# A fused attention and gMLP block on one core: stage-1 loads by need on the SP queue, four-deep key rings, small results on ScalarE

## The chip, the core and the metric

The kernel runs on one core of one Trainium2 chip. The core has five engines with an instruction queue each: TensorE (PE, matmuls; PEld is its weight load), VectorE (DVE), ScalarE (ACT), GpSimd (POOL) and SyncE (SP, which here only issues transfers). ACT can issue transfers too. Transfers run on 16 DMA engines, in one queue row for SP (q1 in the profile) and one for ACT (q10). SBUF is the memory on the core, PSUM holds matmul results. The metric is the device time of one execution in microseconds. Before the change it is 290.84 us, the median of 3 runs (290.23 to 293.64).

## The reference

S = 2048 rows, D = 448, 16 heads of 28, F = 1792; inputs in bfloat16. A condition vector c gives six modulation vectors. Part A is linear attention with softmax features, part B a gMLP with a 2048 x 2048 mixing matrix along the rows.

```python
mod = (_silu(c) @ w_mod).reshape(c.shape[0], 6, 1, -1)      # sa, ca, ga, sb, cb, gb
h = _layernorm(x) * (1 + ca) + sa
q, k, v = heads(h @ wqkv)
phi_k = concat([softmax(k @ w_phi), softmax(-(k @ w_phi))]) # the same for q
kv = einsum('bhsf,bhsd->bhfd', phi_k, v); z = phi_k summed over s
o = (phi_q @ kv) / (phi_q . z + 1e-06)
x = x + ga * (o @ wo)
h = _layernorm(x) * (1 + cb) + sb
zz = _gelu(h @ w_in); z1 = first half; z2 = _layernorm(second half)
g = einsum('ts,bsf->btf', w_sp, z2) + b_sp[None, :, None]
x = x + gb * ((z1 * g) @ w_out)
```

## The kernel before

The rows are 16 tiles of 128. All work stands in one hand-written order; each engine executes its own instructions in that order and waits by semaphores. A second, general path behind a flag is not taken.

**Constants and weights.** The key weights are transposed on PE (`fold_T`, L677), multiplied by w_phi (`fold_pf`, L697) and scaled by 1 + ca on the way out of PSUM (ca1, the second result of `colform`, L708, which multiplies a modulation matrix by silu(c)). `fold_sa` (L689) adds the shift sa as one more column of the transposed weights, copied out by DVE at L695. The same is done for the query weights inside the loop (`late`, L878). `keep_busy` (L624) runs matmuls whose result nobody reads.

**Stage 1**, the loop of L909. For key tile i: `k_part` (L769) multiplies hT (the normalised x, transposed) by the key weights, ACT takes exp(k) and exp(-k) into a ring E of three (L774, L775); `v_part` (L777) does the values, copied by ACT into a second ring; `k_norm` (L783) on DVE sums, inverts and multiplies (L786, L789, L790) into a third ring; `kv_acc` (L794) of tile i-2 adds to the accumulator kvacc in PSUM. For tiles ahead, `l1_stats(i + 6)` (L658) takes mean and variance, on DVE up to tile 9 and on ACT from 10 on; POOL computes the inverse root and applies it (`l1_apply(i + 5)`, L672), and SP transposes the tile by a transfer into hT (L651). `loads(i)` (L843) issues one load per tile on ACT's queue. `late(i)` places the query weights (tiles 1 to 3), the second modulation (tile 5: `one_plus(colform(wm1, 1), cb1)`, then a second `colform`, both in the same PSUM buffer, read by DVE at L717 and L892), the bias products of w_in (`win_bias`, tiles 7 and 8), its scaling on DVE (`win_scale`, tiles 9 to 12) and the gate. Query products `q_mm` (L802) stand behind tiles 9 and 12, and `q_one` (L817) behind the loop; ACT takes exp of both signs.

**PSUM.** Tag B has four banks, tag A two double banks. kvacc holds one of tag A through stage 1. A product waits until the bank that it gets has been read out.

**Stage 2**, `slot(j)` of L1061, j from 0 to 22. In slot j PE makes the attention product of tile j (`num_mm`), DVE finishes tile j-1 (`num_fin`, L972: five operations from L977 to L985, after ACT has copied two sums, `num_sx`, L970), POOL and SP bring it transposed to PE, `wo_mm(j-3)` multiplies by wo and adds x, DVE takes the statistic (L634), POOL applies it for tile j-4 (h2T), and `z2_mm(j-5)` multiplies by the second half of w_in; ACT takes the gelu (L1046) and DVE the statistic (L1008) one slot later. From slot 9 on the first half, `z1`, is multiplied too. The loads of w_sp (`load_wsp`, L826) are transposing transfers on SP, placed in tiles 12 to 14 and slots 5 to 15. The six last `q_one` stand in slots 0 to 5.

**The mixing**, `g_unit` (L1128): 448 matmuls over w_sp, and the output products `o_mm` (L1137), until the end.

## Time and profile before

| | |
|---|---|
| median of 3 runs | 290.84 us (290.23 to 293.64) |
| the profiled execution | 294.1 us, span 292.2 us |
| PE busy | 265.7 us (91%) |
| DVE, ACT, POOL busy | 161.5, 117.2, 90.5 us |
| mean granted clock of PE | 0.948 |

The page cuts the span into 40 equal slices of 7.3 us. Each digit is a share in tenths; PEclk is the granted clock of PE in tenths of full speed (the two levels are 1.2 and 2.4 GHz), DMA the busy share of the 16 DMA engines. Up to slice 15 PE and its clock are uneven, from there on PE is full.

### The profile page before, as it was taken

The page shows a single profiled execution, that of the slowest core. Times are in us where ns is not written, and L with a number is a line of the kernel's source. Part 1 is how long each engine was busy: PE and PEld are TensorE (multiplying, and loading weights), DVE is VectorE, ACT ScalarE, POOL GpSimd, SP SyncE. Part 2 cuts the span into 40 slices and gives each one's busy share as a digit, 9 for nine tenths or more (in the row PEclk, how much of TensorE's full clock was granted, in tenths as well). Part 3 has the DMA queues.
Part 4 walks back from the last instruction along what each step waited for, and adds up shares of the span by engine and source line. Part 5 has one row for each costly group of instructions (what it writes and reads, how often), then busy time and mean ns, then how long its engine had stood idle before and what let it go on. Part 6 is the DMA issues. An engine that isn't in the chain of part 4 may idle for free.

```text
span 292.2 us, 4412 instructions
## 1 busy us (share of the span) xinstructions
PE 265.7 (91%) x1567; PEld 134.3 (46%) x1567; DVE 161.5 (55%) x341; ACT 117.2 (40%) x237; POOL 90.5 (31%) x197
## 2 busy tenths in 40 slices
PE   6795959999995799997999999999999999999991
PEld 3543535556552345554544444444444444444440
DVE  4839645589677489896854324443434353435251
ACT  2347468988972567875788820000000000000000
POOL 3848531330047376774764560000000000000000
PEclk9669777999999789999999999999999999999998
DMA  7679946639012448479734999100000001000002
GB/s 181 154 154 287 160 127 146 92 61 158 0 36 56 91 94 123 96 179 197 109 73 110 185 183 195 17 0 16 18 31 0 16 16 34 0 16 18 31 5 69
DMA packets 71233, 25.82 MB, mean 88 GB/s; under 512 B 61281, under 2 KB 71074, under 8 KB 71202
## 3 DMA queue, kind: packets, MB, share of 16 engines
q1 hardware_dynamic: 63682, 17.79, 33.1%
q10 hardware_dynamic: 7520, 7.66, 10.0%
...
## 4 chain that ended last, share of the span: by engine, by line
PE 58%; DMA 2%; DVE 2%; ACT 1%; issue 1%; ACTq 0%; DVEq 0%
PE g_ps L1132 33%; PE o_ps L1139 7%; PE z_ps L1053 7%; PE z_ps L1040 7%; PE x_ps L998 2%; DMA h2T<-f_xpad 2%; PE num L962 1%; ACT f_z2n L1031 1%; DVE t L985 1%; PE x_ps L996 1%; ACT f_z1T L1054 0%; DVE stats L1008 0%; DVE num L981 0%; DVE cr L977 0%; DVE w L983 0%
## 5 line engine op out<-in xcount | busy, mean ns | idle before, releaser
L1132 PE MATMUL g_ps<-f_wsp,f_z2n 128*128 128x512 bf16 x336 | 74.3, 379 | 0.0
L1132 PEld LDWEIGHTS <-f_z2n 128*128 128x128 bf16 x448 | 43.8, 98 | 52.0
L1134 DVE TENSOR_TENSOR gb<-g_ps,f_bsp 128x512 f32<-128x512 f32 x28 | 19.4, 692 | 70.7 <-PE g_ps L1132 70.7
L1184 ACT CAST ot<-o_ps 128x224 bf16<-128x224 f32 x1 | 0.3, 346 | 116.7 <-PE o_ps L1139 116.7
L1040 PE MATMUL z_ps<-f_win,h2T 128*128 128x448 bf16 (+1 forms) x128 | 28.3, 364 | 4.4 <-DVE t L985 2.6
L1053 PE MATMUL z_ps<-h2T,f_win 128*128 128x512 bf16 x112 | 26.4, 379 | 0.0
L987 POOL TENSOR_TENSOR f_opad<-t 128x448 bf16<-128x448 bf16 x16 | 16.6, 1034 | 27.3 <-DVE t L985 27.3
L1132 PE MATMUL g_ps<-f_hT,f_z2n 128*128 128x512 bf16 x112 | 25.0, 379 | 0.0
L786 DVE TENSOR_REDUCE sums<-f_E 128x32 f32<-128x896 bf16 x16 | 17.2, 1074 | 12.3 <-ACT f_E L775 12.3
L1008 DVE BATCH_NORM_STATS2 stats<-z2g 128x6 f32<-128x448 bf16 x32 | 18.4, 615 | 9.7 <-ACT z2g L1046 9.6
L1139 PE MATMUL o_ps<-f_wout,f_z1T 128*128 128x448 bf16 x112 | 23.5, 352 | 0.0
L1135 DVE TENSOR_TENSOR f_z1T<-gb,f_z1T 128x512 bf16<-128x512 f32 x28 | 19.7, 704 | 1.4
L1046 ACT ACTIVATE z2g<-z_ps 128x896 bf16<-128x896 f32 x16 | 14.7, 918 | 13.0 <-PE z_ps L1040 13.0
L780 PE MATMUL v_ps<-f_Wv,f_hT 128*128 128x448 bf16 x64 | 16.5, 387 | 3.5 <-DVE f_wTq L695 3.5
L1040 PEld LDWEIGHTS <-h2T 128*128 128x128 bf16 (+1 forms) x128 | 12.1, 99 | 15.5 <-issue 3.7
L772 PE MATMUL k_ps<-f_Wk,f_hT 128*128 128x448 bf16 x64 | 18.0, 412 | 1.0 <-DMA f_hT<-f_xpad 0.5
L1031 ACT ACTIVATE f_z2n<-z2g,nm,rs 128x896 bf16<-128x896 bf16 x16 | 18.1, 1132 | 1.6 <-POOL nm L1018 1.4
L985 DVE TENSOR_TENSOR t<-num,w 128x896 bf16<-128x896 f32 x16 | 17.5, 1091 | 1.5
L1053 PEld LDWEIGHTS <-f_win 128*128 128x128 bf16 x112 | 10.9, 97 | 12.6
L998 PE MATMUL x_ps<-f_wo,oT 128*128 128x448 bf16 x64 | 15.6, 369 | 0.8 <-DMA oT<-f_opad 0.8
L824 ACT ACTIVATE f_Eq<-q_ps 112x512 bf16<-112x512 f32 x24 | 12.6, 598 | 8.9 <-PE q_ps L821 8.8
L1139 PEld LDWEIGHTS <-f_z1T 128*128 128x128 bf16 x112 | 11.0, 98 | 10.9
...
## 6 DMA issues: line engine op xcount, KB each, us to landing
...
f_x<-in_A_x_dram ACTq DMA_DIRECT2D x2, 448.0 KB, 4.6
...
```

Source lines behind the costliest of these rows:

```text
L772: nc.tensor.matmul(k_ps[:, 0:D], lhsT=hT[0:KB[kc], kc, i * P:(i + 1) * P], rhs=Wk[0:KB[kc], kc, 0:D], start=(kc == 0), stop=(kc == KC - 1))
L786: nc.vector.tensor_reduce(out=sums[:], in_=E[:].rearrange("p s (c f h) -> p (s c) h f", c=4, h=HP), axis=AX.X, op=ALU.add)
L985: nc.vector.tensor_tensor(out=t[:], in0=nv[:, :, :, 0:DH], in1=w[:].unsqueeze(3).to_broadcast([P, 2, H, DH]), op=ALU.mult)
L998: nc.tensor.matmul(x1[:, 0:D], lhsT=oT[:, cc, :], rhs=wo_s[:, cc, :], start=False, stop=(cc == KC - 1))
L1008: nc.vector.bn_stats(out=stats[:, hf, :], in_=z2gs[i][:, hf, :])
L1031: nc.scalar.activation(out=z2n[:, i, :], in_=z2gs.pop(i)[:].rearrange("p a d -> p (a d)"), func=ACT.Identity, scale=rstd[:, 1:2], bias=nmr ...
L1040: nc.tensor.matmul(z_ps[:, hf, 0:D], lhsT=h2[0:KB[kc], kc, il * P:(il + 1) * P], rhs=win_s[0:KB[kc], kc, FH + hf * D:FH + (hf + 1) * D], s ...
L1053: nc.tensor.matmul(z_ps[:], lhsT=win_s[0:KB[kc], kc, fc * P:(fc + 1) * P], rhs=h2[0:KB[kc], kc, :], start=(kc == 0), stop=(kc == KC - 1))
L1132: nc.tensor.matmul(g[:], lhsT=z2n[:, s_, fc * P:(fc + 1) * P], rhs=wsp_tiles[tcn][:, s_, :], start=(s_ == 0), stop=(s_ == NT - 1))
L1134: nc.vector.tensor_tensor(out=gb[:], in0=g[:], in1=bsp[:, tsl], op=ALU.add)
L1135: nc.vector.tensor_tensor(out=z1T[:, fc, tsl], in0=gb[:], in1=z1T[:, fc, tsl], op=ALU.mult)
L1139: nc.tensor.matmul(o_ps, lhsT=z1T[:, fc, t * P:(t + 1) * P], rhs=wout_s[:, fc, :], start=(first and fc == 0), stop=(fc == FC - 1))
```

## The change

It does the following.

1. **Loads.** The first loads are dealt anew between SP and ACT: w_phi and the first half of the modulation go to SP, the second half to ACT; x rows 4 to 7 and 8 to 11 (tiles) are issued by ACT right after the value weights and after the key fold. The loads of `loads(i)` go from ACT's queue to SP's, one or two per tile, the query weights first.
2. **Rings and lag.** The rings of E, phi_k and v have four buffers (NR = 4), and `kv_acc` runs three tiles behind.
3. **Small results on ACT.** The column of `fold_sa` is copied by ACT in four pieces, into four separate tiles of transposed weights; `colform` puts both results into one bank of tag B, ACT reads them; `fold_T` uses two banks in place of four; half of `win_scale` runs on ACT in pieces of 896 columns.
4. **Places.** `l1_stats` is on DVE up to tile 13. The query fold moves from tiles 1 to 3 to tiles 4 to 6, the second modulation from 5 to 7, the bias products from 7 and 8 to 9 and 10, the scalings to 11 to 14, `q_mm` to 10 and 13. Constants that are used late are written behind the fourth `l1_apply`.
5. **Stage 2.** Its buffers z2n, z1T and the small tiles are allocated over stage 1's before slot 0. `q_one` 10 to 15 stand in slots 0 to 3, the Gelu table is loaded in slot 4, `num_sx` is on DVE for five tiles, `z2_mm` stands ahead of `num_mm` in slots 5 to 8, the statistic behind wo reads x from SBUF. All eight w_sp loads of the first part stand in tiles 11 to 15, those of the second in slots 8 to 15.

```diff
+    NX, NO, NR = 6, 3, 4
+    wTk = [aph.tile([CB, D + 1], BF, name=f"f_wTk{g}") for g in range(4)]
...
     nc.sync.dma_start(out=c_row[:], in_=c)
+    nc.scalar.dma_start(out=x_sb[:, 0:2, :], in_=xv[:, 0:2, :])
+    load_rows(nc.sync, wk_raw[:, :, 0:D], A_wqkv[:, D:2 * D])
+    nc.scalar.dma_start(out=wm1[:, :, D:960], in_=wmod_v[:, :, D:960])
+        nc.sync.dma_start(out=phi[:], in_=A_w_phi.rearrange("(g l) d f -> (l d) g f", l=4))
+    nc.sync.dma_start(out=wm1[:, :, 0:D], in_=wmod_v[:, :, 0:D])
...
     def by_act(i):
-        return i >= 10
+        return i >= 14
...
-        nc.vector.tensor_copy(out=wT[:, :, D], in_=sa_ps[0:CB, 0:4])
+        for g in range(4):
+            nc.scalar.copy(out=wT[g][:, D:D + 1], in_=sa_ps[0:CB, g:g + 1])
...
-    l1_stats(2)
-    fold_T(wk_raw, wTk, (0, 1))
-    one_plus(colform(wm1, 1), ca1)
+    fold_T(wk_raw, wTk, False)
+    cf = colform((1,))
+    nc.vector.tensor_scalar(out=ca1[:], in0=cf[:, 4:8], scalar1=1.0, scalar2=None, op0=ALU.add)
+    nc.vector.memset(ca1[64:65, 3:4], 1.0)
     load_rows(nc.scalar, wv_raw, A_wqkv[:, 2 * D:3 * D])
+    nc.scalar.dma_start(out=x_sb[:, 4:8, :], in_=xv[:, 4:8, :])
     l1_apply(0, nc.vector)
     l1_apply(1, nc.vector)
-    nc.sync.dma_start(out=x_sb[:, 4:8, :], in_=xv[:, 4:8, :])
-    l1_stats(3)
-    l1_rstd(1)
...
-    load_rows(nc.scalar, wq_raw[:, :, 0:D], A_wqkv[:, 0:D])
+    nc.scalar.dma_start(out=x_sb[:, 8:12, :], in_=xv[:, 8:12, :])
...
     def loads(i):
         if i == 0:
-            nc.scalar.dma_start(out=x_sb[:, 8:12, :], in_=xv[:, 8:12, :])
+            load_rows(nc.sync, wq_raw[:, :, 0:D], A_wqkv[:, 0:D])
         elif i == 1:
-            nc.scalar.dma_start(out=wm1[:], in_=wmod_v[:, :, 3 * D:3 * D + 960])
+            nc.sync.dma_start(out=x_sb[:, 12:16, :], in_=xv[:, 12:16, :])
         elif i == 2:
-            load_rows(nc.scalar, win_s[:, :, 0:FH], B_w_in[:, 0:FH])
+            nc.sync.dma_start(out=wm1[:], in_=wmod_v[:, :, 3 * D:3 * D + 960])
         elif i == 3:
-            nc.scalar.dma_start(out=x_sb[:, 12:16, :], in_=xv[:, 12:16, :])
+            load_rows(nc.sync, win_s[:, :, 0:FH], B_w_in[:, 0:FH])
+        elif i == 5:
+            load_rows(nc.sync, win_s[:, :, FH:2 * FH], B_w_in[:, FH:2 * FH])
...
+        if act:
+            nc.scalar.activation(out=w, in_=w, func=ACT.Copy, scale=cb1[0:KD[kk], kk:kk + 1])
...
     def late(i):
+        if i == 4:
+            fold_T(wq_raw, wTq, True)
+        elif i == 5:
             fold_sa(wq_raw, wTq)
...
+        elif i == 7:
+            cf = colform((0, 1))
+            nc.scalar.activation(out=cb1[:], in_=cf[:, 4:8], func=ACT.Identity, bias=1.0)
+            nc.scalar.copy(out=sbpad[:, :, 64], in_=cf[:, 0:4])
+        elif i in (9, 10):
+            win_bias(2 * i - 18)
+            win_bias(2 * i - 17)
+        elif i == 11:
+            gate_rep(0)
+            win_scale(0, False)
+            win_scale(1, True, 0, FH)
...
+    QS = {10: 0, 13: 1}
...
-        if i >= 2:
-            kv_acc(i - 2)
+        if i >= 3:
+            kv_acc(i - 3)
...
+            if i < 5:
+                nc.vector.tensor_copy(out=sxs[i][:, s, :], in_=nv[:, 1 - s, :, 29])
...
-        stats_of(x1s.pop(i)[:, 0:D], mv[:, 0, :], "l2", sm2)
+        stats_of(x_sb[:, i, :], mv[:, 0, :], "l2", sm2)
...
+        if 5 <= j < 9:
+            z2_mm(j - 5)
         if on(j):
             num_mm(j)
...
+    ramp = {0: (10, 11), 1: (12,), 2: (13, 14), 3: (15,)}
+    wsp_rest = [(1, u) for u in range(8)]
+    for j in range(NT + 8):
         slot(j)
+        for n in ramp.get(j, ()):
+            q_one(n)
+        if j == 4:
+            nc.scalar.activation(out=mx[:], in_=mhalf[0:1, 0:1], func=ACT.Gelu_apprx_tanh)
```

The order on SP's queue, first before, from the transpose of tile 1 to that of tile 4 (f_xpad is the normalised tile, f_hT its transposed form, f_x the rows of x):

```order
L651 DMA_TRANSPOSE f_hT<-f_xpad_88 128x4x128
L740 DMA f_x<-in_A_x_dram 128x4x448
L651 DMA_TRANSPOSE f_hT<-f_xpad_89 128x4x128
L651 DMA_TRANSPOSE f_hT<-f_xpad_90 128x4x128
L651 DMA_TRANSPOSE f_hT<-f_xpad_91 128x4x128
```

And now, from the transpose of tile 4 to that of tile 9 (f_wq_raw are the query weights, f_wm the second modulation, f_win the weights of w_in):

```order
L651 DMA_TRANSPOSE f_hT<-f_xpad_91 128x4x128
L561 DMA f_wq_raw<-in_A_wqkv_dram 128x3x448
L562 DMA f_wq_raw<-in_A_wqkv_dram 64x448
L651 DMA_TRANSPOSE f_hT<-f_xpad_92 128x4x128
L848 DMA f_x<-in_A_x_dram 128x4x448
L651 DMA_TRANSPOSE f_hT<-f_xpad_87 128x4x128
L850 DMA f_wm_120<-in_w_mod_dram 112x4x960
L651 DMA_TRANSPOSE f_hT<-f_xpad_88 128x4x128
L561 DMA f_win<-in_B_w_in_dram 128x3x896
L562 DMA f_win<-in_B_w_in_dram 64x896
L651 DMA_TRANSPOSE f_hT<-f_xpad_89 128x4x128
L651 DMA_TRANSPOSE f_hT<-f_xpad_90 128x4x128
```

Before, the load of x was the only one between the transposes, and the rest stood on ACT; now a load stands ahead of nearly each transpose.

The small result of the query fold, before on DVE, between the normalisation of tile 2 and the statistic of tile 9 (f_phik is the normalised key tile, f_wTq the transposed query weights):

```order
L790 TENSOR_TENSOR f_phik_118<-f_E_115,r 128x896
L695 CAST f_wTq<-sa_ps 112x4
L634 BN_STATS stats<-f_x 128x6
L635 BN_AGGR l1mv<-stats 128x2
L786 TENSOR_REDUCE sums<-f_E_113 128x32
```

Now it is on ACT, at tile 5, between that tile's exponentials and the first weights of the query fold:

```order
L775 ACTIVATE f_E_127<-k_ps 128x448
L776 ACTIVATE f_E_127<-k_ps 128x448
L782 CAST f_vaug_135<-v_ps 128x16x28
L696 CAST f_wTq_114<-sa_ps 112x1
L696 CAST f_wTq_115<-sa_ps 112x1
L696 CAST f_wTq_116<-sa_ps 112x1
L696 CAST f_wTq_117<-sa_ps 112x1
L705 ACTIVATE f_Wq<-pf,f_ca_119 128x448 x2
```

One copy behind a normalisation on DVE has become four behind a tile's evacuations on ACT.

The ramp on ACT, before, in slots 4 to 6 (f_Eq are exponentials of the queries, Sx the two sums, z2g the gelu, f_x the new x):

```order
L970 COPY Sx<-num 128x16 x2
L999 CAST f_x<-x_ps 128x448
L824 ACTIVATE f_Eq<-q_ps 112x512 x2
L970 COPY Sx<-num 128x16 x2
L1046 ACT_TABLE_LOAD
L1046 ACTIVATE z2g<-z_ps 128x896
L999 CAST f_x<-x_ps 128x448
```

And now, from slot 3 to slot 6:

```order
L825 ACTIVATE f_Eq<-q_ps 112x512 x2
L1014 CAST f_x<-x_ps 128x448
L1118 ACT_TABLE_LOAD
L1118 ACTIVATE f_mx<-f_mhalf 1x1
L1014 CAST f_x<-x_ps 128x448
L1061 ACTIVATE z2g<-z_ps 128x896
L985 COPY Sx<-num 128x16 x2
```

The last exponentials of the queries and the table load moved ahead of the slots in which gelus run.

## Rows read from the trace of the kernel before

**Rows 1.** Windows by stage: stretch, length, busy time per engine (instructions), PEclk, DMA, GB/s.
```profile
14.00:49.40 35.40, 27.26 (x205) 15.35 (x204) 21.15 (x41) 21.18 (x48) 16.82 (x41) 0.77 0.78 171
49.40:76.30 26.90, 26.82 (x207) 15.51 (x206) 20.58 (x34) 24.37 (x54) 6.25 (x12) 1.00 0.56 97
76.30:111.90 35.60, 29.35 (x192) 15.26 (x191) 24.99 (x66) 21.24 (x52) 18.00 (x31) 0.90 0.32 67
111.90:168.10 56.20, 54.42 (x311) 27.63 (x310) 38.51 (x98) 44.46 (x77) 36.68 (x74) 1.00 0.72 133
```

**Rows 2.** Windows of the low clock up to 50 us, in order PE, PEld, DVE, ACT, POOL.
```profile
9.50:19.40 9.90, 8.48 (x63) 4.46 (x64) 4.58 (x15) 3.88 (x8) 7.52 (x27) 0.50 0.63 153
30.00:33.20 3.20, 3.20 (x21) 2.16 (x21) 2.52 (x5) 0.98 (x2) 2.32 (x5) 0.50 1.02 119
40.60:47.00 6.40, 5.95 (x37) 3.12 (x37) 2.69 (x7) 2.97 (x8) 3.06 (x6) 0.50 0.25 44
```

**Rows 3.** Who waited for whom: total us, times, longest.
```profile
PE v_ps L780 <- DVE f_wTq L695: 3.5, 1, 3.5
PE cf L712 <- DVE f_cb L717: 3.5, 1, 3.5
```

**Rows 4.** Timeline of DVE in stage 1: start us, us, instruction, [idle before, releaser].
```profile
19.74 0.63 DVE L634 BATCH_NORM_STATS2 stats<-f_x 128x6 f32<-128x448 bf16 x1 [4.86 <-DMA f_x<-in_A_x_dram]
...
21.96 1.05 DVE L786 TENSOR_REDUCE sums<-f_E 128x32 f32<-128x896 bf16 x1
...
26.86 0.62 DVE L634 BATCH_NORM_STATS2 stats<-f_x 128x6 f32<-128x448 bf16 x1
...
27.68 1.05 DVE L786 TENSOR_REDUCE sums<-f_E 128x32 f32<-128x896 bf16 x1
...
29.78 0.62 DVE L634 BATCH_NORM_STATS2 stats<-f_x 128x6 f32<-128x448 bf16 x1
```

**Rows 5.** Timeline of PE: one full key tile, and the ends of the stages.
```profile
61.30 0.92 PE L772 MATMUL k_ps<-f_Wk,f_hT 128*128 128x448 bf16 x4
...
62.81 0.58 PE L798 MATMUL kvacc<-f_vaug,f_phik 128*128 128x116 bf16 x8
63.23 1.03 PE L808 MATMUL q_ps<-f_hT,f_Wq 128*128 128x512 bf16 x4
...
75.70 0.59 PE L798 MATMUL kvacc<-f_vaug,f_phik 128*128 128x116 bf16 x8
...
77.86 0.32 PE L962 MATMUL num<-f_KVbd,f_Eq 112*128 112x120 bf16 x3
...
111.88 0.81 PE L1053 MATMUL z_ps<-h2T,f_win 128*128 128x512 bf16 x3
```

**Rows 6.** Timeline of ACT in a full key tile.
```profile
61.19 0.58 ACT L774 ACTIVATE f_E<-k_ps 128x448 bf16<-128x448 f32 x1
...
62.45 0.62 ACT L774 ACTIVATE f_E<-k_ps 128x448 bf16<-128x448 f32 x1
```

**Rows 7.** Timeline of DVE in one slot of stage 2.
```profile
107.24 0.19 DVE L977 TENSOR_TENSOR cr<-num,Sx 128x32 f32<-128x32 f32 x1 [0.17 <-ACT Sx L970]
...
109.28 1.14 DVE L1008 BATCH_NORM_STATS2 stats<-z2g 128x6 f32<-128x448 bf16 x2
...
111.36 0.17 DVE L977 TENSOR_TENSOR cr<-num,Sx 128x32 f32<-128x32 f32 x1
```

**Rows 8.** Windows with the rate of the transfers: the last two numbers.
```profile
20.00:30.00 10.00, 5.88 (x67) 3.82 (x66) 9.55 (x21) 6.24 (x13) 6.44 (x12) 1.00 0.92 237
30.00:40.00 10.00, 7.54 (x68) 4.97 (x68) 5.83 (x10) 6.67 (x16) 3.82 (x7) 0.83 1.04 188
```

**Rows 9.** Transfers on SP: issue of x, its time to landing; transpose of 17.05 to landing.
```profile
13.24 0.57 SPq L740 DMA_DIRECT2D f_x<-in_A_x_dram  x1
...
f_x<-in_A_x_dram SPq DMA_DIRECT2D x1, 448.0 KB, 6.5
...
DMA to landing us min/median/max: 3.3/3.3/3.3
```

More of the change, by code (lines that the diff above doesn't have):

```diff
@@ new lines, in fast_path @@
+    e = aph.tile([DC, KC], F32, name="f_e")
+    warm = aph.tile([P, 1], F32, name="f_warm")
+    sapad = aph.tile([P, KC, P], BF, name="f_sapad")
+    wq_raw = aph.tile([P, KC, D + 16], BF, name="f_wq_raw")
+    wTq = [aph.tile([CB, D + 1], BF, name=f"f_wTq{g}") for g in range(4)]
+    BD = aph.tile([CB, 4, CB], BF, name="f_BD")
+    ca1 = aph.tile([P, KC], F32, name="f_ca1")
+    wm1 = aph.tile([DC, KC, 960], BF, name="f_wm1")
+    scol = aph.tile([DC, KC], BF, name="f_scol")
+    sbpad = aph.tile([P, KC, P], BF, name="f_sbpad")
@@ L581, in fast_path @@
     nc.gpsimd.memset(mhalf[:], -0.5)
-    for r in range(4):
+    nc.gpsimd.memset(sapad[:], 0.0)
+    nc.gpsimd.memset(wv_raw[64:P, 3, :], 0.0)
+    for r in range(NX):
         nc.gpsimd.memset(xpad[r][:, D:512], 0.0)
+    for r in range(NX):
         nc.gpsimd.memset(xpad[r][:, D:D + 1], 1.0)
-    nc.gpsimd.memset(sapad[:], 0.0)
     with nc.allow_low_precision("0/1 masks are exact in bf16"):
@@ L610, in more_constants @@
             nc.gpsimd.memset(opad[r][:, D:512], 0.0)
+        nc.gpsimd.tensor_copy(out=mask16[:], in_=mask[:].unsqueeze(1).to_broadcast([P, 4, HP]))
+        for s in range(2):
+            nc.gpsimd.tensor_copy(out=KVbd[:, s, :, :, 29], in_=mask[:].unsqueeze(1).to_broadcast([P, 4, HP]))
+        nc.gpsimd.tensor_copy(out=scb[:], in_=scol[:].unsqueeze(2).to_broadcast([DC, KC, P]))
     ct_ps = bank_bf("ct_ps")
@@ L677, in fold_T @@
     def fold_T(wraw, wT, act):
-        tps = [bank_bf("tps") for _ in range(4)]
+        tps = [psp.tile([P, 2, 512], BF, name="tps", tag="B", bufs=4) for _ in range(2)]
         for ms in ((0, 1, 2), (3,)):
@@ L706, in fold_pf, with colform @@
             nc.vector.tensor_scalar(out=W[0:M, m, 0:D], in0=pf[0:M, 0:D], scalar1=ca1[0:M, m:m + 1], scalar2=None, op0=ALU.mult)
-    def colform(wm, jv):
-        cf = bank2("cf")[:, 0, :]
-        for m in range(KC):
-            for kk in range(KC):
-                nc.tensor.matmul(cf[:, m:m + 1], lhsT=wm[:, kk, jv * D + m * P:jv * D + m * P + P],
-                                 rhs=scol[:, kk:kk + 1], start=(kk == 0), stop=(kk == KC - 1))
-        return cf
-    def one_plus(cf, dst):
-        nc.vector.tensor_scalar(out=dst[:], in0=cf[:, 0:4], scalar1=1.0, scalar2=None, op0=ALU.add)
-        nc.vector.memset(dst[64:65, 3:4], 1.0)
+    def colform(jvs):
+        cf = bank("cf")
+        for jv in jvs:
+            for m in range(KC):
+                for kk in range(KC):
+                    nc.tensor.matmul(cf[:, jv * 4 + m:jv * 4 + m + 1], lhsT=wm1[:, kk, jv * D + m * P:jv * D + m * P + P],
+                                     rhs=scol[:, kk:kk + 1], start=(kk == 0), stop=(kk == KC - 1))
+        return cf
     def bias_row(pad, W, n0, n1):
@@ L745, in fast_path @@
         fold_pf(wTk, Wk, m, m % 2)
-    cf = colform(wm1, 0)
-    nc.vector.tensor_copy(out=sapad[:, :, 64], in_=cf[:, 0:4])
+    cf = colform((0,))
+    nc.scalar.copy(out=sapad[:, :, 64], in_=cf[:, 0:4])
+    l1_stats(2)
+    l1_stats(3)
+    l1_rstd(1)
     keep_busy(1, 256)
@@ L936, in fast_path @@
             q_mm(QS[i])
-        for u in {12: (0,), 13: (1, 2), 14: (3, 4)}.get(i, ()):
+        for u in {11: (0,), 12: (1, 2), 13: (3, 4), 14: (5, 6), 15: (7,)}.get(i, ()):
             load_wsp(0, u)
+    kv_acc(NT - 3)
     q_one(4)
@@ L969, in num_sx @@
         for s in range(2):
-            nc.scalar.copy(out=sxs[i][:, s, :], in_=nv[:, 1 - s, :, 29])
+            if i < 5:
+                nc.vector.tensor_copy(out=sxs[i][:, s, :], in_=nv[:, 1 - s, :, 29])
+            else:
+                nc.scalar.copy(out=sxs[i][:, s, :], in_=nv[:, 1 - s, :, 29])
     def num_fin(i):
@@ L1054, in z1 @@
         nc.scalar.activation(out=z1T[:, fc, st * 512:(st + 1) * 512], in_=z_ps[:], func=ACT.Gelu_apprx_tanh)
-    z1_split = [(0, 2), (2, 4), (4, 6), (6, 7)]
+    z1_left = [(st, fc) for st in range(4) for fc in range(FC)]
     def on(i):
@@ L1081, in slot @@
             z2_norm(j - 7, j - 1)
-        if 9 <= j < 21:
-            for fc in range(*z1_split[(j - 9) % 4]):
-                z1((j - 9) // 4, fc)
+        for _ in range((2, 2, 2, 1)[(j - 9) % 4] if 9 <= j < 21 else 0):
+            z1(*z1_left.pop(0))
+        if 5 <= j < 9:
+            z2_mm(j - 5)
         if on(j):
             num_mm(j)
-            if j < 3:
-                num_sx(j)
-        if on(j - 5):
+        if on(j - 5) and j >= 9:
             z2_mm(j - 5)
```

174 lines of the change are left out of this document (65 added, 109 removed).

## The prediction

> **What bounds the kernel now.** I read the stages first, then who waits inside them, then single instructions. [rows 1] cuts the execution at five places: the key tiles 0 to 7 with the folding of the weights (14 to 49.4 us), tiles 8 to 15 (to 76.3), the ramp of stage 2 (76.3 to 111.9), stage 2 at full pace (to 168.1), and the last matmuls. The reader is to see where TensorE (PE) is not full or not fast. It is full at clock 1.00 in tiles 8 to 15 (26.82 of 26.90 us) and nearly so from 111.9 to 168.1 (54.42 of 56.20), and behind that stand only the last matmuls, so from 111.9 on only less PE work would help, and the change removes none. The room lies in the first 35.4 us (27.26 busy, clock 0.77) and in the ramp (29.35 of 35.60 busy, clock 0.90). In [rows 2] the granted clock is 0.50, that is the lower level, 1.2 GHz, in three stretches of the first part, each right after PE had stood or worked in fragments.
>
> What PE stood for is in [rows 3]: 3.5 us for a copy of 112x4 numbers (L695) and 3.5 us for an addition on 128x4 (L717). Both results are tiny, and both stand on VectorE (DVE) behind statistics and key normalisation. [rows 4] shows the DVE before that: it stood 4.86 us for a load of x, then ran in a fixed order. Its period for one key tile is 29.78 - 26.86 = 2.92 us, of which 27.68 - 26.86 = 0.82 is the statistic of a later tile and 2.10 the normalisation.
>
> **Stage 1 with the change.** I follow DVE, PE and ScalarE (ACT) apart and take the last.
>
> *DVE.* The x rows 4 to 7 no longer wait on SP's queue behind two transposes, but are issued by ACT right after the value weights, so the 4.86 us should go: the first normalisation moves from 21.96 to about 17.0 [rows 4]. Bounds: no gain, if the rows land as late as now, and 4.86. I take all but little of it, since the issue moves ahead of the transposes for which it waited. Tiles 10 to 13 get their statistics from DVE and no longer from ACT, so tiles 0 to 7 all have the period 2.92: tile 7 is normalised at 17.0 + 2.10 + 7 x 2.92 = 39.5. Tiles 8 to 15 then need 8 x 2.10 = 16.8, to 56.3, and the scaling of four weight pieces behind it.
>
> *PE.* The two stalls of 3.5 us go: the first because ACT now takes the four columns, the second because both column results share one bank and ACT reads them. The four copies that replace one are bounded by nothing and by four exponentials of 0.58 [rows 6], 2.3 us; ACT has that much free in tiles 4 to 7, where DVE's 2.92 per tile sets the pace and an ACT tile costs 62.45 - 61.19 = 1.26. If that cover were gone, 2.3 us would be the price. With the stalls go the low-clock stretches behind them: 3.20 and 5.95 busy us [rows 2] become half. PE's work to tile 8 is then 27.26 - 4.6 = 22.7, less 1.5 for two bias products that move behind tile 8 (each like one group of four matmuls, two groups being 62.81 - 61.30 [rows 5]). From 14 this gives 35.2; I put 36 for tile 8. Bounds: 30.8, when the ring of four lets tile 8 in (17.0 + 2.10 + 4 x 2.92), and 39.5, when tile 7 is normalised. Behind it the 26.9 us full of work [rows 1] grow by those 1.5 and by one accumulation of 0.42 (63.23 - 62.81 [rows 5]), because of the lag of three: 36 + 28.8 = 64.8 for the end of the accumulation, now 75.70 + 0.59 = 76.29 [rows 5].
>
> *ACT.* It gains the statistics of four tiles as free time early, and gets four weight scalings of 896 columns in tiles 11 to 14, where they meet four exponentials over 1024 columns. An ACT tile holds three operations of 448 columns in 1.26 [rows 6], so 1024 columns are 0.96, and I put a scaling at 1.0; tiles 11 to 15 cost 6.3 + 3.8 + 4 + about 1.3 for two small evacuations = 15.4. PE reaches tile 11 at about 36 + 3 x 1.93 + 3 + 1.7 = 46.5 (1.93 = 63.23 - 61.30 per tile [rows 5], 3 for the four bias products, 1.7 for eight matmuls of 512 columns, 2 x 0.75 x 512/448), so ACT ends near 62, and 2.10 of normalisation and an accumulation follow: 64.6. PE and ACT thus end together, and I take 65.0: **11.3 us less**.
>
> *Loads.* In tiles 0 to 9 they move from ACT's queue to SP's, between the transposes of hT, as the order of SP shows. Costed at nothing, because a transpose is issued five tiles ahead. From tile 0 to the transpose of tile 10 the queue carries 392, 448, 840, 784 and 784 KB and six transposes of 128 KB, 4.1 MB. The core moved 237 GB/s from 20 to 30 us and 188 from 30 to 40 [rows 8], with the same kinds of transfer. From about 19.5 us (17.0 on DVE, and POOL's part behind it for tile 4) this is through at 36.8 or at 41.4, and a transpose lands within 3.3 [rows 9]: 40.1 or 44.7, while PE wants tile 10 at about 36 + 2 x 1.93 + 1.5 = 41.4. At the first rate the loads are hidden, at the second they are not.
>
> The same rows show what a load does to a transpose on its own queue: x, issued on SP at 13.24, landed 6.5 us later, at 19.74, and the transpose issued at 17.05 landed after 3.3, at 20.35 [rows 9], so 0.6 behind the load. The Trainium skill, page DMA: Bandwidth & Descriptors, section Queues, rings and completion order, says that each DMA engine takes descriptors in the order of a ring, and goes round between the rows of different issuers; that rule speaks against this change, since a transpose on SP now has all of a load ahead of it, where before it shared the engines with a load of ACT's. The landing just read agrees with it; by that rule the time is the 278 of the forecast while the five tiles of lead last, and that of the second and third rival below when they do not.
>
> *Other moves, at nothing.* Constants on GpSimd (POOL) move behind the fourth apply; POOL is busy 16.82 of 35.4 us there [rows 1]. If the next transpose came late by them, PE would wait at tile 5. Laying stage 2 over stage 1 makes the first small tiles wait for the last normalisation, which comes before the first product of stage 2 anyhow.
>
> **The ramp.** It runs from the end of the accumulation to the first z1, 111.88 - 76.29 = 35.6 [rows 5], of which 34.0 lie behind the first product (77.86). Now two query products stand in slots 3 and 5 and ACT loads its Gelu table in slot 6, in front of the next reader; with the change all query products are out by slot 3 and the table comes in slot 4. What remains is DVE: a slot costs 111.36 - 107.24 = 4.12 once all work runs, of which 109.28 - 107.24 = 2.04 is the finishing of the attention [rows 7] and 0.82 a statistic like those above. The sums that move to DVE add two small copies, 0.4 at the 0.19 of its other small operations there [rows 7]. Slots 0 to 2 are then 2.04 + 0.4 and a little for the query products on PE, 2.6, 2.6 and 3.0; slots 3 to 5 are 2.04 + 0.82 + 0.4 = 3.3, and slots 6 to 8 are 4.12: 30.5 in all. ACT still owes 24 exponentials when the accumulation ends and will be about 1 to 2 late in slot 3. Bounds: 30.5 and the present 34.0, and I take 32.3: **1.7 us less**.
>
> From 111.9 on nothing moves.
>
> **The sum.** 11.3 + 1.7 = 13.0 us. The profiled execution took 294.1 us (span 292.2, and 1.9 around it), so 281.1; its median stands at 290.84 / 294.1 of that, and I predict **278.0 us**. Twelve of the thirteen come from ends that PE, DVE and ACT reach almost together, so a second stall costs at once.
>
> **Rivals.**
> - *The first clock fall goes too* (0.13). PE gets the weights in one piece, and the 8.48 us at 0.50 [rows 2] would become half, 4.2 less. Against it: PE has nothing to do between the transposes of the key weights and the column product in either order, and DVE at 17.0 does not move. I give it 4: 274.
> - *Waits change places in stage 1* (0.20). At 188 GB/s hT of tile 10 lands at 44.7, 3.3 late, and such a stall brings a low-clock stretch like the last one of [rows 2], 5.95 / 2 = 3.0. That takes 6.3 back: 284.3. For it speaks that SP also holds each load until the transposes ahead of it have their POOL result, so that the loads start in gaps; against it that DVE's 2.92 per tile leaves PE late anyhow.
> - *The queue in series, slower than before* (0.12). If each of the five loads takes the 6.5 us that x took [rows 9] and the next starts only behind it, hT of tile 10 lands at 19.5 + 5 x 6.5 + 3.3 = 55.3, 13.9 behind PE. Then the 11.3 are gone, 2.6 come on top, a starved PE runs at the lower level (3.0), and the ramp gives 1.7 back: 3.9 more, 294.7. It decides when that transpose lands after 54. Against it: the 237 GB/s were measured with loads and transposes mixed.
>
> **How the numbers follow.** Forecast 0.55 (273.5 to 283). A measurement of this kernel tells about 2% from no change, so faster means under 285.0: the forecast, the first rival and half of the second, 0.55 + 0.13 + 0.10 = 0.78. Within 2% are the other half and somewhat less than half of the last, 0.15, and 0.07 are left for slower. The range goes from 270 (first rival with the ramp at its lower bound) to 288 (second rival with a second stall), leaving most of the last rival out.
>
> **What the next profile will show.** Right: no wait of PE on DVE in tiles 2 to 6, clock 1.00 from about 20 us on, the first key normalisation near 17, the accumulation ending near 65 and the first z1 near 98, with everything behind it as long as now. Wrong: PE waiting for DMA of hT in tiles 5 to 10 (the queue), ACT without a gap in tiles 11 to 15 and PE waiting for it, or a ramp that is still 34 us. If stage 1 ends at 65 and the whole gains less than 11, the gain was given back behind it, and the forecast's flat tail is wrong.

## The result, and the profile after the change

The changed kernel takes **283.68 us** (median of 4 runs, 282.92 to 284.72) beside 291.56 for the kernel before (4 runs): ratio 0.973, 95% interval 0.965 to 0.980. Timed once more in a later series it took 283.31 beside 294.46, ratio 0.961 (0.953 to 0.969). I had forecast 278.0 in a range of 270 to 288. Executions of one program differ by some per cent (the kernel before: 289.2 to 298.6 in 13 runs of one series), so the experiments below are read stage by stage in their traces, and the times stand beside.

The profiled execution took 283.17 us, with a span of 281.3. First the page's slices of 7.0 us, to be read like those of before:

```profile
PE   7579999999939799989999999999999999999991
PEclk9869999999998999979999999999999999999997
```

PE is full from the fourth slice on but for one hole in the twelfth; before, it was uneven up to the fifteenth. The stages, cut at the same five events as [rows 1] (columns: stretch, its length, busy us and instructions of PE, PEld, DVE, ACT and POOL, PE's granted clock, DMA share, GB/s):

```profile
15.35:36.11 20.76, 20.09 (x189) 12.15 (x189) 17.54 (x33) 15.95 (x39) 15.48 (x34) 0.92 0.88 196
36.11:64.93 28.82, 28.61 (x221) 16.78 (x222) 22.25 (x38) 26.39 (x55) 6.56 (x12) 1.00 0.89 169
64.93:98.74 33.81, 27.42 (x192) 14.88 (x191) 24.88 (x72) 20.57 (x44) 17.74 (x30) 0.95 0.24 44
98.74:156.81 58.07, 56.02 (x310) 28.03 (x309) 39.28 (x102) 44.58 (x77) 36.60 (x75) 0.97 0.68 130
156.81:281.30 124.49, 118.43 (x563) 54.79 (x561) 47.83 (x74) 1.96 (x3) 4.87 (x5) 0.99 0.19 39
```

Tiles 0 to 7 take 20.76 us in place of 35.40, tiles 8 to 15 take 28.82 in place of 26.90 (they now hold the bias products), and the ramp 33.81 in place of 35.60. The fourth row is the surprise: 58.07 us at clock 0.97, where [rows 1] has 56.20 at 1.00. What PE waited for (the list of waits: us, times, longest):

```profile
PE z_ps L1055 <- DMA h2T<-f_xpad: 5.5, 2, 4.3
PE k_ps L773 <- DMA f_hT<-f_xpad: 3.8, 2, 3.6
PE ct_ps L616 <- DMA f_c_row<-in_c_dram: 2.0, 1, 2.0
PE z_ps L1055 <- DVE w L998: 1.7, 1, 1.7
```

The two waits of 3.5 us of [rows 3] are gone. What is left are transposed tiles that land late: the first hT, and h2T of tile 0 in the ramp. Now single instructions of PE and DVE that answer to [rows 4] and [rows 5] (start, us, engine, line, operation; in brackets the idle time ahead and what ended it):

```profile
15.35 3.17 PE L773 MATMUL k_ps<-f_Wk,f_hT 128*128 128x448 bf16 x8 [3.64 <-DMA f_hT<-f_xpad]
36.11 0.93 PE L773 MATMUL k_ps<-f_Wk,f_hT 128*128 128x448 bf16 x4 [0.20 <-DMA f_hT<-f_xpad]
64.35 0.58 PE L799 MATMUL kvacc<-f_vaug,f_phik 128*128 128x116 bf16 x8
66.50 0.58 PE L974 MATMUL num<-f_KVbd,f_Eq 112*128 112x120 bf16 x8
82.97 2.75 PE L1055 MATMUL z_ps<-f_win,h2T 128*128 128x448 bf16 x8 [4.33 <-DMA h2T<-f_xpad]
120.89 3.11 PE L1055 MATMUL z_ps<-f_win,h2T 128*128 128x448 bf16 x8 [1.67 <-DVE w L998]
```

```profile
13.54 0.63 DVE L634 BATCH_NORM_STATS2 stats<-f_x 128x6 f32<-128x448 bf16 x1 [1.02 <-DMA f_x<-in_A_x_dram]
18.07 1.09 DVE L787 TENSOR_REDUCE sums<-f_E 128x32 f32<-128x896 bf16 x1 [2.23 <-ACT f_E L776]
37.92 1.05 DVE L787 TENSOR_REDUCE sums<-f_E 128x32 f32<-128x896 bf16 x1
```

Tile 8 begins at 36.11 and the accumulation ends at 64.93; the first z1 stands at 98.74. At 82.97 and 120.89 PE comes out of a wait with the clock down: the eight matmuls take 2.75 and 3.11 us, where they take 1.68 elsewhere.

### The profile page after: what moved, and what is told of

The parts are those of the page before. It is cut to its first block, busy times and chain, and to the rows that moved or that the text cites. A ratio compares the mean times of both kernels' runs of the same rounds, so it can differ in the third digit from the quotient of the medians.

```text
span 281.3 us, 4413 instructions
## 1 busy us (share of the span) xinstructions
PE 259.6 (92%) x1567; PEld 132.5 (47%) x1567; DVE 161.4 (57%) x349; ACT 114.2 (41%) x227; POOL 89.5 (32%) x201
## 3 DMA queue, kind: packets, MB, share of 16 engines
q10 hardware_dynamic: 3744, 3.62, 4.9%
## 4 chain that ended last, share of the span: by engine, by line
PE 75%; DVE 8%; DMA 8%; ACT 3%; issue 2%; POOL 1%; SPq 0%; DVEq 0%; POOLq 0%; ACTq 0%
PE g_ps L1142 34%; PE z_ps L1055 8%; PE o_ps L1149 8%; PE z_ps L1068 7%; DMA f_hT<-f_xpad 5%; PE q_ps L822 3%; PE k_ps L773 3%; PE x_ps L1013 3%; PE v_ps L781 2%; DMA f_phi<-in_A_w_phi_dram 2%; PE num L974 2%; DMA h2T<-f_xpad 2%; DVE t L1000 2%; PE kvacc L799 1%; PE q_ps L809 1%
## 5 line engine op out<-in xcount | busy, mean ns | idle before, releaser
L1055 PE MATMUL z_ps<-f_win,h2T 128*128 128x448 bf16 (+1 forms) x128 | 29.4, 376 | 7.7 <-DMA h2T<-f_xpad 5.5
L773 PE MATMUL k_ps<-f_Wk,f_hT 128*128 128x448 bf16 x64 | 16.1, 380 | 3.9 <-DMA f_hT<-f_xpad 3.8
L634 DVE BATCH_NORM_STATS2 stats<-f_x 128x6 f32<-128x448 bf16 x30 | 17.9, 597 | 2.2 <-ACT f_x L1014 1.2
L1069 ACT ACTIVATE f_z1T<-z_ps 128x512 bf16<-128x512 f32 x28 | 15.1, 588 | 0.4 <-PE z_ps L1068 0.4
L1013 PE MATMUL x_ps<-f_wo,oT 128*128 128x448 bf16 x64 | 14.9, 355 | 0.1
```

Of the source, the lines that this page charges most:

```text
L634: nc.vector.bn_stats(out=stats[:], in_=src)
L773: nc.tensor.matmul(k_ps[:, 0:D], lhsT=hT[0:KB[kc], kc, i * P:(i + 1) * P], rhs=Wk[0:KB[kc], kc, 0:D], start=(kc == 0), stop=(kc == KC - 1))
L1013: nc.tensor.matmul(x1[:, 0:D], lhsT=oT[:, cc, :], rhs=wo_s[:, cc, :], start=False, stop=(cc == KC - 1))
L1055: nc.tensor.matmul(z_ps[:, hf, 0:D], lhsT=h2[0:KB[kc], kc, il * P:(il + 1) * P], rhs=win_s[0:KB[kc], kc, FH + hf * D:FH + (hf + 1) * D], s ...
```

## The experiments

This table cuts every profiled execution at the same events: the end of the accumulation, then from the first product to the first z1 (ramp), from there to the first product of the mixing (full pace), and from there to the end. The last column is PE's wait for h2T in slot 13 of stage 2, where the stretch at full pace has its one large stall, and whether the clock was 0.50 behind it.

| kernel | accumulation ends | ramp | full pace | rest | stall in slot 13 |
|---|---|---|---|---|---|
| before | 76.29 | 34.02 | 56.05 | 124.27 | 1.78, no fall |
| before again (E5) | 74.69 | 32.72 | 60.27 | 123.75 | 3.48, fall |
| changed | 64.93 | 32.24 | 58.07 | 124.49 | 1.67, fall |
| changed again (E12) | 65.47 | 32.98 | 56.18 | 124.20 | 1.68, no fall |
| E1 output weights later | 65.15 | 32.67 | 54.56 | 124.05 | none |
| E2 product first in slot 5 | 65.86 | 27.98 | 59.93 | 124.16 | 3.40, fall |
| E3 small results on DVE | 66.77 | 30.48 | 60.02 | 124.26 | 3.62, fall |
| E4 before, small results on ACT | 70.71 | 34.18 | 61.78 | 123.86 | 3.29, fall |
| E6 x on SP | 70.63 | 32.40 | 60.11 | 123.99 | 3.85, fall |
| E7 rings of three | 66.53 | 32.47 | 59.46 | 124.17 | 3.26, fall |
| E8 loads on ACT | 69.77 | 32.67 | 56.14 | 123.96 | 1.41, no fall |
| E9 both edits | 66.54 | 27.97 | 54.67 | 124.45 | none |
| E10 both, and filler matmuls | 65.72 | 29.45 | 54.67 | 124.59 | none |
| E11 before, output weights later | 74.18 | 33.32 | 54.02 | 123.81 | none |

Five executions hold the changed stage 1 (changed, E12, E1, E2, E9): it ends at 64.9 to 66.5, 65.6 in the mean. Three hold that of before (before, E5, E11): 74.2 to 76.3, 75.1 in the mean. The five ends come in the order in which PE's clock rose from 0.50 to 1.00 behind the first key products, which start at 15.3 to 15.7 in all of them: between 18.5 and 19.0 us in the changed kernel (end 64.93), at about 20.5 in E1 (65.15), between 20.5 and 21.0 in E12 (65.47), 21.5 and 22.0 in E2 (65.86), 22.0 and 22.5 in E9 (66.54). So an end that is 1 us later says little by itself; below it is also compared with an execution whose clock rose at the same moment.

### Where the gain went behind the ramp: E1, E11, E5, E12

**E1.**

```diff
-        if j == 12:
+        if j == 20:
             nc.scalar.dma_start(out=wout_s[:], in_=B_w_out...)
```

> The changed kernel with one edit: the load of the output weights (784 KB, ACT's queue) is issued in slot 20 of stage 2 in place of slot 12. In the changed kernel the transposed tile h2T issued at 114.55, right behind that load at 114.27, landed after 6.3 us where the median is 2.5, PE stood 1.67 us from 119.2, and the clock was 0.50 from 121 to 124, where 2.9 us of work cost 1.4 more. Theory (the load delays the transpose, and the clock falls after the stall): the stall and the low-clock stretch behind it both go, first z1 to first product of the mixing shrinks from 58.07 to 54.5 to 55.5, and the kernel takes 280.0 to 281.2 instead of 283.7. Rival (the transposed loads of the mixing weights on SP's own queue delay it, so the stall stays): 58 stays and the time changes by less than 0.7.

It took 280.9 us (280.04 to 283.86), ratio to before 0.970 (0.954 to 0.986). In the changed kernel the load and the transpose meet like this (SP's and ACT's issues, then the time from issue to landing of that one transpose):

```profile
114.27 0.37 ACTq L1126 DMA_DIRECT2D f_wout<-in_B_w_out_dram  x1
114.55 1.21 SPq L651 DMA_TRANSPOSE h2T<-f_xpad  x1
DMA to landing us min/median/max: 6.3/6.3/6.3
```

114.55 + 6.3 = 120.85, and PE starts at 120.89: the wait that the list puts down to DVE is this transpose. In E1 the stretch is full, at clock 1.00:

```profile
99.39:153.95 54.56, 54.18 (x311) 27.54 (x310) 39.17 (x102) 44.62 (x77) 34.39 (x72) 1.00 0.68 123
```

The theory holds: the stretch is 3.5 us shorter than in the first profile of the changed kernel, and 1.6 shorter than in its second (E12). The time alone does not show it, since the ratios to before, 0.970 and 0.973, lie inside each other's intervals.

**E11** makes the same edit in the kernel before.

> The kernel before with the load of the output weights in slot 20 and nothing else. Before carries the same stall in slot 13: 1.78 us without a fall of the clock in the first profile (stretch from first z1 to the mixing 56.05), 3.48 with seven slow microseconds in the second (60.27). Theory (the stall is in both kernels, of a size that differs between executions, so that the profile from which the forecast was made had little of it): stretch 54 to 55, span about 288 to 291, and time 286 to 289.5. Rival (it is of the changed kernel alone): nothing changes, 290 to 293.

It took 290.13 us beside 293.36, 3.2 less, ratio 0.992 (0.988 to 0.997): clear of 1, though under 2% and just above the 286 to 289.5 of the theory. The stretch is 54.02, as the theory said: the stall belongs to both kernels. In the first profile of before it looks like this (ACT's issue of the load, then PE; the transpose issued at 127.90 landed after 5.7 us, at 133.6):

```profile
126.90 0.38 ACTq L1117 DMA_DIRECT2D f_wout<-in_B_w_out_dram  x1
133.69 1.69 PE L1040 MATMUL z_ps<-f_win,h2T 128*128 128x448 bf16 x8 [1.78 <-DMA h2T<-f_xpad]
```

**E5** and **E12** profile both kernels again, unchanged.

> The kernel before, unchanged, profiled once more. The forecast scaled its sum by the median of before over its profiled execution, 290.84 / 294.1, as if the 3.3 us above the median lay evenly over the program. Theory (what differs between executions is a transpose that is late behind a load, with the clock behind it, and not an even share): end of the accumulation and the ramp come out within 1 us of 76.29 and 34.02, the last matmuls at 124 to 124.5, and the stretch from first z1 to the first product of the mixing, 56.05 in the first profile, anywhere from 55 to 62. Rival (an even share): every stretch moves in the same proportion.

> The changed kernel, unchanged, timed and profiled once more beside the kernel before. Theory (a fixed part of the gain lies in the accumulation's end and the ramp, and what differs between executions is the stall in slot 13): end of the accumulation 64.9 to 66.6, ramp 32 to 33, last matmuls 123.9 to 124.5, the stretch from first z1 to the mixing anywhere from 56 to 60.2, time 282.5 to 286. Rival (the first profile of the changed kernel was a lucky one elsewhere): the end of the accumulation beyond 67 or the ramp beyond 33.5.

E5 was 294.91 us. Its stage 1 ended 1.6 earlier than in the first profile and its ramp was 1.3 shorter, each a little beyond the 1 us I had allowed, and its stretch at full pace was 4.2 longer; an even share would have moved all one way. Its stall in slot 13:

```profile
132.41 3.17 PE L1040 MATMUL z_ps<-f_win,h2T 128*128 128x448 bf16 x8 [3.48 <-DMA h2T<-f_xpad]
131.00:137.40 6.40, 4.99 (x14) 2.09 (x15) 1.48 (x3) 0.92 (x1) 1.94 (x4) 0.50 1.03 163
```

E12 fell inside its expectation everywhere. So the profile that the forecast was built on had a late stage 1, and little of this stall.

### The ramp: E2, and both edits: E9

**E2** turns the order in slot 5, and lets DVE copy the sums of tile 5.

```diff
-        if 5 <= j < 9:
+        if 6 <= j < 9:
             z2_mm(j - 5)
         if on(j):
             num_mm(j)
-        if on(j - 5) and j >= 9:
+        if on(j - 5) and (j == 5 or j >= 9):
...
-            if i < 5:
+            if i < 6:
                 nc.vector.tensor_copy(out=sxs[i][:, s, :], ...)
```

> The changed kernel with slot 5 of the ramp in another order: the attention product of tile 5 ahead of the first product of the second half (z2_mm(0)), and its two sums copied by DVE. In the changed kernel z2_mm(0) stands first and waits 4.33 us for h2T of tile 0 (78.64 to 82.97), and DVE has nothing for 4.46 us because the attention product stands behind it. Theory (the order of slot 5 gave back part of the ramp): DVE finishes tile 5 inside the wait, each later slot starts up to 3 us earlier, the ramp from first product to first z1 shrinks from 32.2 to 29 to 30.5 and the kernel takes 281 to 282. Rival (the later slots are paced by the chain from h2T of tile 0 on, which does not move): less than 0.7 us.

```profile
81.36 0.59 PE L974 MATMUL num<-f_KVbd,f_Eq 112*128 112x120 bf16 x8
82.65 1.68 PE L1055 MATMUL z_ps<-f_win,h2T 128*128 128x448 bf16 x8 [0.70 <-DVE t L1000]
119.41 1.88 PE L1055 MATMUL z_ps<-f_win,h2T 128*128 128x448 bf16 x8 [3.40 <-DMA h2T<-f_xpad]
```

The product of tile 5 stands at 81.36 (in the changed kernel at 85.52, behind z2_mm(0)), z2_mm(0) runs at 1.68 us, and the ramp is 27.98: more than I had expected. The kernel took 281.49 (279.33 to 283.56), ratio 0.965 (0.944 to 0.987); the last row shows why not less: the wait in slot 13 ate part of it. That time alone would not tell it from the changed kernel, whose ratio is 0.973; the ramp does. **E9** makes both edits.

> The changed kernel with two edits together: the load of the output weights in slot 20, and the attention product of tile 5 ahead of z2_mm(0) in slot 5 with its sums on DVE. Apart, the first took the stretch from first z1 to the mixing from 58.07 to 54.56, and the second took the ramp from 32.24 to 27.98 while that stretch grew to 59.93, because its transpose was still caught by the load (3.40 us). Theory (the two gains are independent): ramp 28, stretch 54.5, span 65.5 + 1.6 + 28 + 54.5 + 124.2 = 273.8, time 275 to 277. Rival (the earlier ramp only meets the next transfer): one of the two stretches stays, 279 or more.

It took **276.33 us** (275.5 to 277.11), ratio to before 0.944 (0.935 to 0.953), and its slowest run lies below the fastest of the changed kernel in any series (281.6); ramp 27.97 and stretch 54.67, so the two gains are independent.

### What stage 1 owes to each part: E3, E4, E6, E7, E8

**E3** puts the small results of the loop back on DVE; **E4** takes them to ACT in the kernel before and changes nothing else there.

```diff
-            fold_sa(wq_raw, wTq)            # columns read by ACT
+            fold_sa(wq_raw, wTq, True)      # columns read by DVE
...
-            nc.scalar.activation(out=cb1[:], in_=cf[:, 4:8], func=ACT.Identity, bias=1.0)
-            nc.scalar.copy(out=sbpad[:, :, 64], in_=cf[:, 0:4])
+            nc.vector.tensor_scalar(out=cb1[:], in0=cf[:, 4:8], scalar1=1.0, ...)
+            nc.vector.tensor_copy(out=sbpad[:, :, 64], in_=cf[:, 0:4])
```

> The changed kernel with the small results of the loop back on DVE: the four columns behind the query weights' shift at tile 5, and the two column results of the second modulation at tile 7. Everything else stays (x loaded early, rings of four, loads on SP). Theory of the forecast (a tiny copy behind a key normalisation stalls PE): DVE is at the normalisation of tile 5 from 32.2 to 34.3 when PE wants the columns at about 30.5, so PE stands about 3.5 us, a low-clock stretch follows, and the end of the accumulation moves from 64.9 to 68.5 to 72; the kernel takes 287 to 290. Rival (the rings of four and the early x are what took the stalls away): PE waits under 1 us, the end stays under 66 and the time within 0.7 of the changed kernel.

> The kernel before with one part of the change alone: the columns of the query weights' shift at tile 2 and the two column results at tile 5 are read out by ACT in place of DVE. Rings of three, lag of two, x rows 4 to 7 on SP and all loads stay. Theory (the two stalls of 3.5 us hung on DVE's order alone): both go with the low-clock stretches behind them, up to 11 us, but DVE still starts its first normalisation at 22 and the ring of three holds PE at tile 8 until about 38.5; the accumulation ends near 66 to 69 in place of 76.3, and the kernel takes 281 to 285. Rival (without the early x and the fourth buffer PE waits at the ring instead): the end stays at 72 or later and the kernel takes 287 to 291.

E3's four runs lie at 280.5 to 287.6 (median 286.1), too far apart to read a gain from; its wait at this place is

```profile
PE pf L702 <- DVE f_wTq L696: 1.0, 1, 1.0
```

with no slow stretch behind it, and the accumulation ends at 66.77, 1.2 beyond the mean of the changed kernel and 1.3 beyond E12, whose clock rose in the same half microsecond. Neither theory hit: DVE does read the columns 4.4 us after PE has made them (34.75, against 30.31 for the first of them), as I had said, but in the new place only the one product that needs the column waits, and not the value product for its bank, as at L695 before. E4's accumulation ended at 70.71, 4.3 earlier than the mean of before and later than I had expected, because one stall stayed:

```profile
PE cf L712 <- ACT f_cb L890: 3.7, 1, 3.7
```

The two results still share one buffer there, and ACT reads the first only behind two statistics and a tile's three evacuations, and had stood 1.56 us ahead of them (30.72 to 32.28) with a load issued in between. E4's time, 292.28 beside 292.92, ratio 1.001 (0.994 to 1.007), lies outside both expectations and shows none of it: in the profiled execution the stretch at full pace was 61.78, the longest of all. Its trace has, beside the 3.29 us in slot 13, a second wait of PE for h2T, 1.21 us at 160.64, which no other has there; why that tile came late, and why the other runs were no faster, stays open.

**E6** issues x rows 4 to 7 on SP behind two transposes; **E7** takes rings of three and a lag of two; **E8** issues the loop's loads on ACT.

```diff
-    nc.scalar.dma_start(out=x_sb[:, 4:8, :], in_=xv[:, 4:8, :])
     l1_apply(0, nc.vector)
     l1_apply(1, nc.vector)
+    nc.sync.dma_start(out=x_sb[:, 4:8, :], in_=xv[:, 4:8, :])
```

> The changed kernel with x rows 4 to 7 issued by SP behind the transposes of tiles 0 and 1, as before. Theory of the forecast (DVE sets the pace of tiles 0 to 7): the first normalisation goes from 18.1 back to about 22, and all of the 3.9 us arrive at the end of the accumulation, 68.8. Rival (with a lag of three PE has slack there: in the changed kernel the normalisation of tile 6 ends at 37.2, and PE uses it at 39.6, 2.4 later, the smallest distance of tiles 0 to 7): the end moves by 1.5 or less, 65 to 66.5, and the first hT, which then shares the engines with less, lands up to 1.4 earlier.

> The changed kernel with rings of three and a lag of two, as before; all else stays. By the rows of the changed kernel PE reaches the accumulation of tile i-2 in tile i 0.3 to 0.5 us behind the end of its normalisation in tiles 4 to 8 (34.25 against 34.55 in tile 7), and 0.5 ahead of it in tile 9. Theory (the fourth buffer and the lag of three carry nothing by themselves once DVE is early): end of the accumulation 64.5 to 66. Rival (they take up the jitter between DVE and PE, and without them the low clock comes back): end at 67 or later, with a stretch at 0.50 between 20 and 50 us.

> The changed kernel with the loads of the loop issued by ACT again, each in the same tile as now. The forecast costed their move at nothing. Theory (loads hidden on either queue): end of the accumulation within 0.7 of 64.9; the transpose of tile 8, which landed after 6.6 us behind the load of w_in on its own queue and let PE wait 0.2, lands sooner. Rival (SP's queue is what keeps ACT's exponentials on time, or the transposes early): the end moves by 1.5 or more.

*E6* (290.57 us, one run) ended stage 1 at 70.63, 5.0 beyond the mean, 1.8 beyond the 68.8 of the forecast's theory, and on another path than that theory's. DVE is 2.45 later (20.52 against 18.07), and PE waits for no normalisation; it waits for hT, in tiles 5 to 8:

```profile
29.25 0.93 PE L773 MATMUL k_ps<-f_Wk,f_hT 128*128 128x448 bf16 x4 [1.29 <-DMA f_hT<-f_xpad]
32.48 0.93 PE L773 MATMUL k_ps<-f_Wk,f_hT 128*128 128x448 bf16 x4 [0.33 <-DMA f_hT<-f_xpad]
37.14 0.93 PE L773 MATMUL k_ps<-f_Wk,f_hT 128*128 128x448 bf16 x4 [2.15 <-DMA f_hT<-f_xpad]
41.82 0.93 PE L773 MATMUL k_ps<-f_Wk,f_hT 128*128 128x448 bf16 x4 [1.78 <-DMA f_hT<-f_xpad]
```

The statistic is the first link of statistic, POOL, transpose. The one that waits for x starts at 18.30 in place of 13.54, and the transposes of tiles 5 to 8 are issued 4.35 to 5.20 us later than in the changed kernel, while they land after 2.4, 3.0, 5.8 and 8.0 us, where it has 2.4, 3.1, 5.5 and 6.6. So what x loses there uses up the lead that the transposes need. PE waiting for hT is what the forecast's second rival had, but by the rate of the transfers; here the transposes go out late, and the early x is what kept that away. It has a price: without it the first key product stands at 13.96, with it at 15.35. *E7* (286.16, one run) ended at 66.53, 0.9 beyond the mean, and 0.7 beyond E2, whose clock rose in the same half microsecond, with PE waiting 0.2 us for a normalisation and no slow stretch behind 22 us. E9 ended as late without this edit, so that the fourth buffer and the lag of three are worth a microsecond at most, and perhaps nothing.

*E8* (286.22, one run) ended at 69.77, 4.2 beyond the mean: the rival. ACT in tile 3 (the load's issue, and the exponential behind it), then PE:

```profile
29.48 0.38 ACTq L561 DMA_DIRECT2D f_win<-in_B_w_in_dram  x1
30.53 0.55 ACT L775 ACTIVATE f_E<-k_ps 128x448 bf16<-128x448 f32 x1 [4.10 <-DVE l1mv L635]
31.56 1.42 PE L773 MATMUL k_ps<-f_Wk,f_hT 128*128 128x448 bf16 x4 [2.56 <-ACT f_E L776]
```

ACT stood 4.10 us, not for work but for the load that it had to issue. In the program's order that load has a wait of its own:

```
L561 DMA f_win_72<-in_B_w_in_dram 128x3x896 [waits DMAHW2_49]
```

In this program eight such semaphores go round over the transfers of SP and ACT together; the one before on this number is the transpose of tile 5, which SP issued at 22.53 and which landed 6.9 us later:

```profile
L651 SPq DMA_TRANSPOSE f_hT<-f_xpad x1: 1342/1342/1342, 22.5 to 22.5; - x1
DMA to landing us min/median/max: 6.9/6.9/6.9
```

22.53 + 6.9 = 29.43, and the load was issued at 29.48. So a load on ACT's queue made ACT, and the exponentials behind it, wait for a transpose of SP's; on SP's queue it makes only SP wait, and the transposes behind it. In the three profiles with the stage 1 of before, whose loads are on ACT too, ACT never stood longer than 1.13 us at a load: the 4.10 is the price of loads on ACT in the changed kernel, and not one that the kernel before paid. The landing times of the key transposes between 8 and 50 us also differ, changed kernel first, E8 second:

```profile
DMA to landing us min/median/max: 2.3/3.8/7.0
```

```profile
DMA to landing us min/median/max: 2.3/6.2/8.4
```

But in E8 PE waits for no hT behind the first, so the longer landings cost it only what came through that semaphore; the 2.56 us and the low clock behind them (0.56 from 31.5 to 34.5) are most of the 4.2. And the queue alone does not set the landing: the median is 4.1 and 4.2 in the two profiles of before, loads on ACT, and 4.2 in E7, loads on SP.

### The first fall of the clock: E10

```diff
     keep_busy(2, 256)
+    keep_busy(16)
```

> The kernel with both edits, and 16 more matmuls of 512 columns that nobody reads, in front of the first key product, where PE stands 3.6 us for the first hT in the changed kernel (11.7 to 15.35) and the clock is 0.50 until 18.7 to 21.7. Theory (the chain from DVE over POOL and SP to hT sets the pace there, not PE): the clock stays at 1.00, the first exponentials come 0.8 earlier since one key product takes 0.92 in place of 1.69, and the accumulation ends 0.5 to 1.2 earlier than in the kernel with both edits. Rival (PE alone sets the pace): what the low clock cost, 1.7 to 3.2, comes back whole. Second rival (the clock falls there whatever PE does): nothing changes.

```profile
11.98 4.98 PE L627 MATMUL warm_ps<-f_sbpad,f_ident 128*128 128x256 bf16 x18
16.79 1.68 PE L774 MATMUL k_ps<-f_Wk,f_hT 128*128 128x448 bf16 x8
36.91 0.93 PE L774 MATMUL k_ps<-f_Wk,f_hT 128*128 128x448 bf16 x4 [0.92 <-DMA f_hT<-f_xpad]
14.50:23.00 8.50, 8.10 (x42) 3.91 (x41) 5.56 (x12) 4.33 (x10) 7.93 (x20) 1.00 0.69 149
```

The clock is back at 1.00 from 14.5 us, eight key matmuls take 1.68 us in place of 3.17, and the accumulation ends 0.8 earlier than in E9, as the first theory said; tile 8 now waits 0.92 for its hT. Since E9 is the latest of the five and E10's 65.72 lies inside their 64.9 to 66.5, this confirms little. And the filler, begun at the low clock, took 4.98 us (two older matmuls included) and pushed the first key product 1.25 later than in E9, so the experiment does not price a fall that never comes. The time, 276.86 (276.09 to 281.26), is that of E9.

## Why the prediction was right in direction and 5.7 us too low

**Stage 1, forecast end 65.0: right, 64.93.** The early x took the wait of 4.86 to 1.02. The first normalisation came at 18.07, not at 17.0, since the first hT landed late and DVE waited 2.23 for the exponentials; the period was (37.92 - 18.07) / 7 = 2.84 for 2.92; tile 8 stood at 36.11 for 36, by two differences that cancel: the first key product came at 15.35 and not at 14, which by E6 the early x itself caused, and tiles 0 to 7 took 20.76 for 22. The end itself varies between 64.9 and 66.5, and that of before between 74.2 and 76.3, so the 11.3 of the forecast are 9.5 in the mean.

**What the forecast credited in stage 1: partly wrong.** It gave the two stalls and their slow stretches to the small results on ACT. Undoing each part in the changed kernel costs, against the mean of 65.6: x 5.0, loads on SP 4.2, small results 1.2, rings and lag 0.9, each by one profile, the last inside the spread of the five. These sum to 11.3 beside the 9.5, but parts that lean on each other need not add up, and these do: the small results alone gained 4.3 in the kernel before (E4), and E8's wait of ACT is no part of the time before. The loads' move, "costed at nothing", was worth 4.2 us with the other parts in place. It was hidden (PE waited 0.20 for hT of tile 8), but my question was only whether a transpose would suffer on SP, not what the loads did to ACT.

**The rule that spoke against the loads on SP.** In the single case the rows agree: the transpose of tile 8 went out at 29.43 behind the load of w_in, and PE started on it at 36.11. Over all key transposes the rule does not come out: they landed after 3.8 us in the median, against 6.2 in E8 and 4.1 in the kernel before, both with the loads on ACT. The Trainium skill, page DMA: Bandwidth & Descriptors, section Queues, rings and completion order, has both sides: order on one ring, and turns between the rows of two issuers. E8's longer landings would fit the second, while the 4.1 does not ask for it; no run takes them apart further.

**The ramp, forecast 32.3: right by luck, 32.24.** The products of slots 0 to 5 stand at 66.50, 68.66, 70.70, 74.61, 76.85 and 85.52. Slots 0 to 3 took 10.35 for 11.5, slot 4 took 8.67 for 3.3, because z2_mm(0), now ahead of the product, waited for h2T, and the last four, to z1, 13.2 for 15.7. The list of the change names that new order, but the forecast's sum gave it no wait; E2 shows that it cost 4.3.

**"From 111.9 on nothing moves": this step failed.** The stretch at full pace took 58.07 for 56.05 and the rest 124.49 for 124.27, together 2.2. The changed kernel does not cause it: the load of the output weights catches a transpose in slot 13 in both kernels, for 1.4 to 3.9 us, and the clock falls behind it or not. The profile of before held 1.78 without a fall. I had read its 54.42 of 56.20 as full and passed over the 1.78.

**The last step of the sum failed too, by 3.1.** The 281.1 of the sum were right for the profiled execution but for those 2.2 (283.17). I then multiplied by 290.84 / 294.1, taking the profiled execution of before for a slow one on the word of three runs. Later series of before have medians of 292.9, 293.4 and 294.5 (single runs go from 289.2 to 298.6): it was an ordinary one. 2.1 from the first to the profile, 3.1 of scale and 0.5 from there to the median are the 5.7.

**The rivals.** The first clock fall did not go (0.51 from 12 to 18.7), and the queue in series did not come. The second rival's wait was there with 0.20 us in place of 3.3; E6, without the early x, has 5.6 us of it over four tiles.
